# A Fourier mixing layer and an MLP in one kernel: outputs of a pair of products one product later, the last stage's first splits tied to tiles 10 to 12, and one block's scale from ScalarE's sums

## The chip, the cores and the metric

The kernel runs on one core of a Trainium2 chip. That core has a matrix engine (TensorE, in the profile PE for its matmuls and PEld for its weight loads), three engines for elementwise work (VectorE or DVE, ScalarE or ACT, GpSimd or POOL) and SyncE (SP), which only issues transfers here. Every engine works through its own queue in order. The metric is the device time of one execution in microseconds; the time before is 1283.4 us, the median of 3 runs (1282.92 to 1283.59).

## What is computed

The input x has 2048 rows of 576 numbers. It is normalized row by row, and the result goes through a Fourier mixing layer and an MLP, whose outputs are added to x:

```
xn = layernorm(x)
a  = xn @ dft_hid_re.T          b = xn @ dft_hid_im.T
y  = dft_seq_re @ a - dft_seq_im @ b        # 2048 x 2048 matrices
h  = relu(xn @ w1)                          # 576 -> 4608
out = x + y + h @ w2                        # 4608 -> 576
```

All data are float32.

## The kernel before

**Numbers as two halves.** TensorE works on float16. Each float32 operand is scaled by a power of two and split in a high half (ScalarE, a copy to float16) and a low half (VectorE, the scaled value minus the high half). A product of two such operands is three matmuls: low by high, high by high, high by low. `split` (lines 182 and 183) is this pair of instructions. The scale of an operand comes from its largest value, or from a sum of absolute values, which bounds it: from VectorE's reduction (`magnitude`, L115) or from ScalarE's accumulator (`sum_w1`, L578; `sum_w2`, L604). `power_pe` finds the maximum over partitions with two small matmuls (L158 and L166), `power` does it with GpSimd.

**Strassen's scheme.** Most large products are done as 2 x 2 blocks with seven products P1 to P7 in place of eight; the sums and differences that this needs are VectorE's work.

**The stages.** First a prologue loads x, normalizes and transposes it and starts the MLP. Then the main loop goes over 9 blocks of w1 and w2 (512 hidden units each) and, in each block, over 4 groups of 512 rows. Blocks 0 and 1 form the hidden values with plain products (L310). From block 2 on, 28 steps form them as two "pairs" of seven products each (`pair_products`, L440): the loop names them first and second. A product's result lies in one of four PSUM banks. Some products have a copy or an add that frees the bank for the next one (the table `free`, L466 to L471), and some have outputs that are not needed in this step (the table `use`): `value`, L447 and L448, makes the two halves of an output, P3 finishes r21 (L476), P4 makes A12 and the four sums (L451 to L454). Two more instructions split these sums at the end: L459 on ScalarE and L462 on VectorE, held in a list `ends`. Between those products stand the seven products of the second matrix (`mlp2`, L510) of the step before, which read the hidden values h; L519 and L521 take their results out, and GpSimd adds them to DRAM (L523). After the MLP comes the hidden transform, 16 tiles of 128 rows (`dft1`, L1002 and L1012), whose results are split into R (L1022 to L1034). The last stage multiplies the 2048 x 2048 matrices with R: 16 units of seven products (L1116), each with an operand of 128 x 1024 that `operand` forms by adds and subtracts (L1063 to L1068) and a split.

**Preparing.** A list `todo` holds small steps of preparation: for each block of weights the loads, the scale, the sums and the splits; before the last stage `power_c` (the scale), `load_c(0)` and the first three operands. `work()` takes one entry off, and the loops call it at fixed places (`ready` in the paired steps; once after each tile from tile 2 on in the transform). A second list, `passes`, loads each block of the 2048 x 2048 matrices once ahead of time and sums its absolute values on ScalarE (L874), one entry at each `count`.

**What sets the order.** The builder lays out each engine's queue before the run. It goes through the instructions on its own model of the machine: an engine that is free there takes, among those that are ready by that model, the one that stands first in the program's text. So an instruction can run ahead of its place in the text where the model saw the engine idle. `tc.issue_after(ins)` forbids that: what is traced inside it on the engine of `ins` comes behind `ins` in the queue. The dictionary `order` keeps the instructions used for this: `order["s"]` and `order["lo"]` are the last closing splits (L459 and L462 in the paired steps), `order["acc"]` is the last accumulation (L521).

The order of a paired step is written out by hand as a list of (what, which) in lines 919 to 927.

Of the kernel before, what the change touches and what calls it, by code (L numbers as in the profile page):

```python
# [2 lines left out]

# [6 lines left out]
F16 = mybir.dt.float16  # L10
F32 = mybir.dt.float32
BF16 = mybir.dt.bfloat16
I32 = mybir.dt.int32
AF = mybir.ActivationFunctionType
ALU = mybir.AluOpType
# [3 lines left out]
P = 128  # L19
# [11 lines left out]
GH = G // 2  # L31
KT = 5
# [10 lines left out]
BB = 2  # L43
# [6 lines left out]
def kernel(  # L50
# [17 lines left out]
    nc = tc.nc  # L68

    const = ctx.enter_context(tc.tile_pool(name="const", bufs=1))  # L70
    small = ctx.enter_context(tc.tile_pool(name="small", bufs=2))
# [3 lines left out]
    mlp = tc.alloc_tile_pool(name="mlp", bufs=2)  # L75
# [17 lines left out]
    raws = {}  # L93
# [19 lines left out]
    def magnitude(dst, src):  # L113

        nc.vector.tensor_reduce(dst, src, AX.XY, ALU.max, apply_absolute_value=True)  # L115
# [72 lines left out]
    means, factors, shifts, order = {}, {}, {}, {}  # L188
# [115 lines left out]
    w1s, w2s, us, hs = {}, {}, {}, {}  # L304
    w1bufs = [mlp.tile([P, W1B], F32, name=f"w1buf{i}", bufs=1) for i in range(2)]
# [61 lines left out]
    P1, P2, P6, P5, P7, P3, P4 = range(7)  # L367
# [161 lines left out]
    sc, pw, mx = {}, {}, {}  # L529

    def max_w1(b, f):

        i, r = divmod(f, 2)
        if f == 0:
            mx["w1", b], sc["w1", b], pw["w1", b] = cell("mw1"), cell("sw1"), cell("pw1")
        if r == 0:
            mx["f", b] = cell("mf", 2)
            mx["b", i] = small.tile([P, 1], BF16, tag=f"mb{i}", name=f"mb{b}_{i}")
        with tc.issue_after(order["lo"]) if b else nullcontext():
            magnitude(mx["f", b][:, r : r + 1], raws["w1", b, i][:, r * KT : (r + 1) * KT])  # L540
        if r:
            nc.vector.tensor_reduce(mx["b", i], mx["f", b], AX.X, ALU.max)

# [28 lines left out]
    def sum_w1(b, i):  # L572

        if i == 0:
            mx["w1", b], sc["w1", b], pw["w1", b] = cell("mw1"), cell("sw1"), cell("pw1")
        w = w1bufs[b % 2 * 2 + i].bitcast(F16)
        w1s[b, i] = w.rearrange("p (n k f) -> p n k f", n=2, f=P)
        nc.scalar.activation(  # L578
            w[:, : 2 * KT * P].rearrange("p (k f) -> p k f", f=P), raws["w1", b, i], AF.Abs,
            scale=2.0**-10, accum_out=mx["w1", b][:, i : i + 1],  # L580
        )

    def sums_w1(b, i):
        r = raws["w1", b, i]
# [65 lines left out]
    def prepare_w1(b, i):  # L650
        p = power_w1(b, i)
        if b < BB:
            return [
                lambda: max_w1(b, 2 * i),
                lambda: max_w1(b, 2 * i + 1),
                lambda: later(p),
            ], [
                lambda: split_w1(b, 2 * i),
                lambda: split_w1(b, 2 * i + 1),
            ]  # L660
        return [
            lambda: (sum_w1(b, i), next(p)),
            lambda: None,
            lambda: later(p),
        ], [
            lambda: split_w1b(b, i, 0),
            lambda: split_w1b(b, i, 1),
            lambda: sums_w1(b, i),
            lambda: split_w1b(b, i, 2),
            lambda: split_w1b(b, i, 3),  # L670
        ]
# [91 lines left out]
    w = prepare_w2(0)  # L763
# [118 lines left out]
    for n in range(2, len(steps)):  # L882
        b, g = steps[n]
        pb, pg = steps[n - 1]
        if g == 0 and b:
            if b + 1 < NB:
                todo += prepare_block(b + 1)
            else:
                todo += [lambda: (load_d(0), load_d(1)), lambda: None, new_d, lambda: None]
                for j in range(4):  # L890
                    d = power_d(j)
                    todo += [lambda d=d: next(d), lambda d=d, j=j: (later(d), split_d(j))]
                    if j < 2:
                        todo += [lambda j=j: load_d(j + 2), lambda: None]
                todo += [scales_d]
        if b == 0 and g + 1 < NG:
            with tc.issue_after(order["lo"]):
                weave(stats([(g + 1) * TG + i for i in range(TG)]))
        if b == NB - 1 and g:

            size = 2 * EH
            if g == 1:
                w = mlp.tile([P, 2, 7, EH], F16, tag="w2s", name="sums", bufs=4)
                w = [w.rearrange("p n q e -> p (n q e)").bitcast(F32)]
            elif g == 2:
                w = [raw.tile([P, KT, EH], F32, tag="raw", name=f"sums{k}") for k in range(2)]
                w = [r.rearrange("p k e -> p (k e)") for r in w]
            sumbufs[:] = [
                r[:, k : k + size].rearrange("p (c e) -> p c e", e=EH)
                for r in w for k in range(0, r.shape[1] - size + 1, size)  # L910
            ]
        if b >= BB:
            first, second = (pair_products(b, g, i) for i in range(NQ))
            later1, later2 = (lambda q, f=f: f(q, True) for f in (first, second))
            m = lambda q: mlp2(pb, pg, q)
            end = lambda q: ends and ends.pop(0)()
            ready = lambda q: [work() for _ in range(q)]
            count = lambda q: n > 3 and passes and passes.pop(0)()
            for do, q in (
                (first, P1), (first, P2), (m, 0), (end, 0), (first, P6), (ready, 1),  # L920
                (first, P5), (later1, P2), (ready, 1), (m, 1), (end, 0), (second, P1), (ready, 1),
                (first, P7), (m, 2), (second, P2), (later1, P7), (ready, 1),
                (first, P3), (first, P4), (count, 0), (later1, P3), (m, 3), (later1, P4), (second, P6),
                (later2, P2), (ready, 1), (m, 4), (end, 0), (second, P5), (ready, 1), (m, 5), (end, 0),
                (second, P7), (ready, 1), (m, 6), (ready, 2), (second, P3), (later2, P7),
                (count, 0), (second, P4), (later2, P3), (later2, P4), (ready, 1),
            ):
                do(q)
            for _ in range(4):
                next(tq, None)  # L930
            continue
        ps = []
        for i in range(NF):
            if n == 2:
                ps.append(early.pop(0) if early else mlp1(b, g, i))
            else:
                mlp1_step(b, g, i, ps)
            if i % 2:
                mlp1_out(b, g, i // 2, *ps[i - 1 : i + 1])
            if b == 0 and g + 1 < NG:  # L940
                t = (g + 1) * TG + i
                normalize(t)
                remainder(t, nc.gpsimd)
                transposes(t)
            if n == 2 and i == 2:
                todo += prepare_block(1)
            for _ in range(1 if b else 3):
                work()
            for q in range(2 * i, min(2 * i + 2, 7)):
                mlp2(pb, pg, q)  # L950
                if b:
                    next(tq, None)
            if b and i == 3:
                next(tq, None)
            for _ in range(1 + i % 2 if b else 3):
                work()
            if n > 3 and i % 2 and passes:
                passes.pop(0)()
# [30 lines left out]
    def dft1(t):  # L989
# [40 lines left out]
            nc.scalar.activation(hi, src, AF.Copy, scale=r)  # L1030
            stt(lo, src, r, hi, ALU.mult, ALU.subtract)  # L1031
        hi, lo = (R[t][:, n, T3 : T2 + 1] for n in range(2))
        nc.scalar.activation(hi, T, AF.Copy)
        nc.vector.tensor_tensor(lo, T, hi, ALU.subtract)  # L1034

    A = {}

    def load_c(n):
        pool = cr[n % 2]
        for q, src in enumerate(blocks_c(n)):  # L1040
            r = A[n, q] = pool.tile([P, HK, P], F32, tag=f"c{q}", name=f"c{q}_{n}")
            nc.sync.dma_start(r, src)
# [13 lines left out]
    def operand(m):  # L1056

        n, i = divmod(m, 7)
        q = PRODUCTS[i][0]
        a11, a22, a12, a21 = (A[n, j] for j in range(4))  # L1060
        tt = nc.vector.tensor_tensor
        if q == S2:
            tt(a21, a21, a22, ALU.add)  # L1063
            tt(a11, a21, a11, ALU.subtract)
        elif q == S3:
            tt(a21, a22, a11, ALU.subtract)
        elif q == S4:
            tt(a12, a12, a11, ALU.subtract)  # L1068
        src = {A11: a11, A22: a22, A12: a12, S1: a21, S2: a11, S3: a21, S4: a12}[q]
        w = csp[m] = cs.tile([P, 2, HK, P], F16, tag="cs", name=f"cs{m}")  # L1070
        split(w[:, 0], w[:, 1], src, sc["c"][:, n : n + 1])

    todo += [power_c, lambda: None, lambda: load_c(0)] + [lambda: None] * 8
    todo += [lambda m=m: operand(m) for m in range(3)]
    for t in range(NT):
        if t and t % TG == 0:
            xpool[t // TG - 1].release()
# [104 lines left out]
```

## Time and profile before

| | |
|---|---|
| median of 3 runs | 1283.4 us |
| the profiled execution | 1285.6 us |
| its span, first to last instruction | 1283.8 us |
| mean granted TensorE clock | 0.995 |
| paired steps (blocks 2 to 8) | about 206 to 836 us |
| transform | about 836 to 949 us |
| last stage | about 949 us to the end |

The profile comes from one execution. A row of a group of instructions gives line, engine, operation, what it writes and reads, shapes and count, then busy time and mean duration, then the engine's idle time just before these instructions and what ended it. A row of the timeline gives start, length and instruction, with the idle time before it in brackets. A row of the waits gives who waited for whom, the total in us, how often, and the longest. A row of windows gives for each stretch the busy time of each engine with its count of instructions, the granted clock of TensorE and the transfers' share. Matmuls are pipelined: their number in a stretch says more about TensorE's pace than its busy time.

### The profile page before, as it was taken

The numbers are of one execution on the slowest core, as the hardware profiler recorded it, in microseconds if no ns is written. First come the engines' busy times: TensorE is split into PE (matmuls) and PEld (weight loads), VectorE is DVE, ScalarE is ACT, GpSimd is POOL, SyncE is SP. The second block draws the span as 40 slices with busy tenths as digits, with TensorE's granted clock in tenths as the row PEclk, the third lists the DMA queues.
The fourth block names the chain that finished last, engine by engine and source line by source line (L and its number), as shares of the span: only waits on it lengthen the run. The fifth ranks groups of instructions, "written<-read, shape, count | busy, mean of one in ns | idle before, by whom it ended". The sixth has DMA issues, their size and how long they took to land.

```text
span 1283.8 us, 25483 instructions
## 1 busy us (share of the span) xinstructions
PE 1247.0 (97%) x10396; PEld 990.4 (77%) x10396; DVE 1002.9 (78%) x1879; ACT 727.8 (57%) x1218; POOL 149.0 (12%) x188
## 2 busy tenths in 40 slices
PE   7899999999999999999999999999999999999998
PEld 7665566888888888878878887867777777777776
DVE  8989998786877776777867877567668788888875
ACT  5835567676776676766766765544443333333332
POOL 2320012111112121211121111100000000000000
PEclk9899999999999999999999999999999999999999
DMA  6112457566756675666666665630033435344320
GB/s 242 43 62 69 124 124 153 131 116 142 146 131 122 133 149 121 133 136 126 120 142 143 138 135 121 111 94 17 1 124 113 153 105 165 117 127 135 127 85 20
DMA packets 60806, 150.75 MB, mean 117 GB/s; under 512 B 6288, under 2 KB 21136, under 8 KB 60688
## 3 DMA queue, kind: packets, MB, share of 16 engines
q1 hardware_dynamic: 42256, 111.36, 27.1%
q0 software_dynamic: 18432, 37.76, 20.9%
q8 instruction: 81, 1.33, 0.4%
q14 instruction: 37, 0.30, 0.1%
HBM read 101.91 MB, written 47.19 MB: 116 GB/s over the span
## 4 chain that ended last, share of the span: by engine, by line
PE 69%; DVE 17%; ACT 5%; DMA 5%; issue 3%; SPq 1%; POOL 0%; ACTq 0%; POOLq 0%; DVEq 0%
PE p L1116 25%; PE p L510 17%; PE bank L440 17%; PE pd L1002 7%; DMA raw_w<-in_w_dram 2%; DVE w2s L183 2%; PE p L310 2%; ACT h L459 1%; DVE h L448 1%; DVE h L462 1%; ACT f L874 1%; DMA c<-in_cim_dram 1%; DMA c<-in_cre_dram 1%; DVE dbuf L183 1%; DVE w1buf L183 1%
## 5 line engine op out<-in xcount | busy, mean ns | idle before, releaser
L510 PE MATMUL p<-w2s,h 128*128 128x288 f16 x3024 | 409.8, 286 | 4.7 <-DVE acc L521 2.0
L510 PEld LDWEIGHTS <-h 128*128 128x128 f16 x3024 | 295.0, 98 | 81.3 <-issue 6.1
L1116 PE MATMUL p<-R,cs 128*128 128x288 f16 x2688 | 329.6, 286 | 1.8 <-DVE o L1122 1.8
L1116 PEld LDWEIGHTS <-cs 128*128 128x128 f16 x2688 | 263.0, 98 | 68.2 <-issue 2.0
L182 ACT ACTIVATE cs<-c,sc_c 128x1024 f16<-128x1024 f32 x112 | 128.5, 1148 | 205.1 <-PE p L1116 151.3
L183 DVE SCALAR_TENSOR_TENSOR cs<-c,sc_c,cs 128x1024 f16<-128x1024 f32 x112 | 143.7, 1283 | 50.9 <-ACT cs L182 50.8
L440 PEld LDWEIGHTS <-w1buf 128*128 128x128 f16 x1600 | 156.4, 98 | 30.4 <-issue 9.3
L440 PEld LDWEIGHTS <-dbuf 128*128 128x128 f16 x1200 | 117.3, 98 | 22.7 <-issue 7.0
L440 PE MATMUL bank<-xT,w1buf 128*128 128x256 f16 x832 | 109.8, 273 | 1.9 <-ACT acc L469 1.9
L1002 PE MATMUL pd<-dbuf,xT 128*128 128x288 f16 x832 | 106.0, 289 | 2.4 <-DVE R L1031 2.4
L440 PE MATMUL bank<-acc,w1buf 128*128 128x256 f16 x768 | 102.1, 272 | 4.6 <-DVE acc L470 2.9
L462 DVE TENSOR_TENSOR h<-s,h 128x1024 f16<-128x1024 f32 x56 | 68.5, 1224 | 48.4 <-ACT h L459 48.4
L1002 PEld LDWEIGHTS <-xT 128*128 128x128 f16 x832 | 81.5, 99 | 25.8 <-issue 4.8
L523 POOL DMA_DIRECT2D spill<-dbuf x74 | 64.1, 868 | 291.9 <-DVE dbuf L521 225.8
L440 PE MATMUL bank<-xT,dbuf 128*128 128x256 f16 x624 | 82.3, 273 | 1.6 <-ACT acc L469 1.6
L447 ACT ACTIVATE h<-acc 128x256 f16<-128x256 f32 x112 | 46.3, 414 | 59.9 <-DVE acc L470 43.6
L440 PE MATMUL bank<-acc,dbuf 128*128 128x256 f16 x576 | 76.6, 272 | 3.1 <-ACT s L468 1.7
L448 DVE SCALAR_TENSOR_TENSOR h<-acc,h 128x256 f16<-128x256 f32 x112 | 47.3, 423 | 35.1 <-ACT h L447 34.8
L1122 DVE SCALAR_TENSOR_TENSOR o<-p,us_c,o 128x288 f32<-128x288 f32 x112 | 57.5, 514 | 20.3 <-PE p L1116 20.3
L459 ACT ACTIVATE h<-s 128x1024 f16<-128x1024 f32 x56 | 59.0, 1053 | 20.9 <-DVE s L454 19.6
L874 ACT ACTIVATE f<-f 128x1024 f32<-128x1024 f32 x64 | 67.1, 1049 | 5.1 <-DMA f<-in_cre_dram 5.1
L519 ACT ACTIVATE dbuf<-p,c_ub 128x576 f32<-128x576 f32 x74 | 54.1, 732 | 21.4 <-ACT h L447 11.3
(158 smaller groups left out, 1538.7 us busy)
## 6 DMA issues: line engine op xcount, KB each, us to landing
spill<-dbuf POOLq DMA_DIRECT2D x74, 288.0 KB, 5.2
f<-in_cre_dram SPq DMA_DIRECT2D x32, 512.0 KB, 4.5
f<-in_cim_dram SPq DMA_DIRECT2D x32, 512.0 KB, 3.7
c<-in_cre_dram SPq DMA_DIRECT2D x32, 512.0 KB, 4.6
c<-in_cim_dram SPq DMA_DIRECT2D x32, 512.0 KB, 4.8
spill<-sum POOLq DMA_DIRECT2D x38, 288.0 KB, 5.2
raw_w<-in_w_dram SPq DMA_DIRECT2D x17, 640.0 KB, 5.0
raw_w<-in_w_dram SPq DMA_DIRECT2D x18, 576.0 KB, 3.8
```

What stands on the lines that cost most here:

```text
L182: nc.scalar.activation(hi, src, AF.Copy, scale=s)
L183: nc.vector.scalar_tensor_tensor(lo, src, s, hi, ALU.mult, ALU.subtract)
L440: nc.tensor.matmul(ps, l, r, start=first and m == 0, stop=m == len(todo) - 1, skip_group_check=not first,)
L448: stt(lo, src, 0.0, hi, ALU.max, ALU.subtract)
L459: order["s"] = nc.scalar.activation(hi_s, st[:, 1:], AF.Copy).ins
L462: order["lo"] = nc.vector.tensor_tensor(lo_s, st[:, 1:], hi_s, ALU.subtract).ins
L510: nc.tensor.matmul(ps[:, c], h[:, x, qa, c * P : (c + 1) * P], w[:, y, qb], start=first and i == 0 and j == 0, stop=i == NQ - 1 and j == 2 ...
L523: nc.gpsimd.dma_start(spill[g, row, col], o, accum_op=ALU.add)
L874: nc.scalar.activation(f, f, AF.Abs, scale=2.0**-10, accum_out=sums_c[:, n, q : q + 1])
L1002: nc.tensor.matmul(ps[j], xT[g][:, kx, c * P : (c + 1) * P], dsp[j][:, hl, k], start=(t % 2 == 0 and n == 0), stop=(t % 2 == 1 and n == le ...
L1116: nc.tensor.matmul(ps, w[:, a, k], r[:, c, rq], start=first and k == 0 and j == 0, stop=k == HK - 1 and j == 2, skip_group_check=not first,)
L1122: nc.vector.scalar_tensor_tensor(o, ps, us["c"][:, n : n + 1], o, ALU.mult, ALU.add)
```

## The change

Three places change.

The scale of block 1's w1 no longer comes from VectorE's two reductions per half (`max_w1`), which stood behind `order["lo"]`, but from `sum_w1`, so far used from block 2 on; in block 1 it writes its junk output to a tile of the ring "stage", and a copy to bfloat16 hands the sums to `power_pe`. The preparing list keeps its length.

In the paired step, the outputs of the first pair (`later1`) and of the second (`later2`), the closing splits (`end`) and the second `count` change places with products and preparing entries.

In the transform, each tile now records its closing splits in `order`, the empty entries ahead of the first three operands go from 8 to 5, and those operands are tied behind the closing splits of the tile after which they are called.

```diff
 def max_w1(b, f):
-        with tc.issue_after(order["lo"]) if b else nullcontext():
-            magnitude(mx["f", b][:, r : r + 1], raws["w1", b, i][:, r * KT : (r + 1) * KT])
+        magnitude(mx["f", b][:, r : r + 1], raws["w1", b, i][:, r * KT : (r + 1) * KT])
...
 def sum_w1(b, i):
-        w = w1bufs[b % 2 * 2 + i].bitcast(F16)
-        w1s[b, i] = w.rearrange("p (n k f) -> p n k f", n=2, f=P)
+        if b < BB:
+            junk = mlp.tile([P, 5, GH], F32, tag="stage", name=f"j1_{b}_{i}")
+            junk = junk.rearrange("p a b -> p (a b)")
+        else:
+            junk = w1bufs[b % 2 * 2 + i].bitcast(F16)
+            w1s[b, i] = junk.rearrange("p (n k f) -> p n k f", n=2, f=P)
         nc.scalar.activation(
-            w[:, : 2 * KT * P].rearrange("p (k f) -> p k f", f=P), raws["w1", b, i], AF.Abs,
+            junk[:, : 2 * KT * P].rearrange("p (k f) -> p k f", f=P), raws["w1", b, i], AF.Abs,
             scale=2.0**-10, accum_out=mx["w1", b][:, i : i + 1],
         )
+        if b < BB:
+            mx["b", i] = small.tile([P, 1], BF16, tag=f"mb{i}", name=f"mb{b}_{i}")
+            nc.vector.tensor_copy(mx["b", i], mx["w1", b][:, i : i + 1])
...
 def prepare_w1(b, i):
-                lambda: max_w1(b, 2 * i),
-                lambda: max_w1(b, 2 * i + 1),
+                lambda: sum_w1(b, i),
+                lambda: None,
                 lambda: later(p),
...
                 (first, P1), (first, P2), (m, 0), (end, 0), (first, P6), (ready, 1),
                 (first, P5), (later1, P2), (ready, 1), (m, 1), (end, 0), (second, P1), (ready, 1),
-                (first, P7), (m, 2), (second, P2), (later1, P7), (ready, 1),
-                (first, P3), (first, P4), (count, 0), (later1, P3), (m, 3), (later1, P4), (second, P6),
-                (later2, P2), (ready, 1), (m, 4), (end, 0), (second, P5), (ready, 1), (m, 5), (end, 0),
-                (second, P7), (ready, 1), (m, 6), (ready, 2), (second, P3), (later2, P7),
-                (count, 0), (second, P4), (later2, P3), (later2, P4), (ready, 1),
+                (first, P7), (m, 2), (second, P2), (ready, 1), (first, P3), (first, P4), (count, 0),
+                (later1, P7), (m, 3), (second, P6), (later1, P3), (later1, P4), (later2, P2),
+                (ready, 1), (m, 4), (second, P5), (ready, 1), (m, 5), (end, 0), (second, P7),
+                (end, 0), (ready, 1), (m, 6), (count, 0), (ready, 2), (second, P3), (second, P4),
+                (later2, P7), (later2, P3), (later2, P4), (ready, 1),
...
 def dft1(t):
-        nc.scalar.activation(hi, T, AF.Copy)
-        nc.vector.tensor_tensor(lo, T, hi, ALU.subtract)
+        order["s"] = nc.scalar.activation(hi, T, AF.Copy).ins
+        order["lo"] = nc.vector.tensor_tensor(lo, T, hi, ALU.subtract).ins
...
-    todo += [power_c, lambda: None, lambda: load_c(0)] + [lambda: None] * 8
-    todo += [lambda m=m: operand(m) for m in range(3)]
+    todo += [power_c, lambda: None, lambda: load_c(0)] + [lambda: None] * 5
+    def first_operand(m):
+        with tc.issue_after(order["s"]), tc.issue_after(order["lo"]):
+            operand(m)
+
+    todo += [lambda m=m: first_operand(m) for m in range(3)]
```

More of the change, by code (lines that the diff above doesn't have):

```diff
@@ L1 @@
 import itertools
-from contextlib import ExitStack, nullcontext
+from contextlib import ExitStack
 import concourse.bass as bass
```

## The prediction

> **What bounds the kernel now.** I read the page first: its span, the engines' shares, and its stages by windows; then the list of waits on TensorE, and last the timeline wherever that list names a place. The page:
>
> ```profile
> span 1283.8 us, 25483 instructions
> ...
> PE 1247.0 (97%) x10396; PEld 990.4 (77%) x10396; DVE 1002.9 (78%) x1879; ACT 727.8 (57%) x1218; POOL 149.0 (12%) x188
> ```
>
> TensorE is busy for 1247.0 of 1283.8 us, so whatever this change can win lies in 36.8 us of idle time and in any slow matmuls; no edit adds or removes work of TensorE. Three stages hold the edits of loop and last stage (window, its length, PE busy, PEld, DVE, ACT, POOL, granted clock, DMA share, GB/s):
>
> ```profile
> 206.00:750.00 544.00, 535.43 (x4588) 448.52 (x4587) 410.97 (x905) 377.74 (x733) 93.37 (x119) 1.00 0.65 135
> 750.00:836.00 86.00, 83.26 (x711) 69.09 (x710) 60.52 (x125) 50.70 (x93) 16.65 (x20) 1.00 0.58 116
> 836.00:949.00 113.00, 110.64 (x906) 84.73 (x904) 77.32 (x129) 50.53 (x81) 2.62 (x3) 0.98 0.12 32
> ```
>
> The paired steps (206 to 836) idle TensorE 8.6 + 2.7 = 11.3 us, the transform (836 to 949) 2.4 us at a clock below 1.00. TensorE's waits by releaser (total, times, longest):
>
> ```profile
> PE bank L440 <- DVE acc L470: 4.0, 8, 1.4
> PE bank L440 <- ACT acc L469: 3.5, 5, 1.1
> ...
> PE pd L1002 <- DVE R L1031: 2.4, 3, 1.3
> PE bank L440 <- ACT s L468: 2.2, 3, 1.2
> ...
> PE p L1116 <- DVE o L1122: 1.8, 1, 1.8
> PE p L310 <- ACT xT L265: 1.5, 2, 1.2
> ...
> PE pm L158 <- DVE mb L614: 0.4, 1, 0.4
> ...
> PE pm L158 <- DVE mb L542: 0.2, 1, 0.2
> ```
>
> L440 is the paired steps' products, L1002 the transform, L1116 the last stage; L310 and L158 are the first products and the scales of blocks 0 and 1.
>
> **Part 1, the last stage's first splits.** Their 3 entries come after 5 empty ones instead of 8, so in the text they move from tiles 13, 14, 15 to tiles 10, 11, 12; and they may no longer run ahead of that place. Today they do. The timeline at the transform's start:
>
> ```profile
> 848.75 1.15 ACT L182 ACTIVATE cs<-c,sc_c 128x1024 f16<-128x1024 f32 x1 [2.81 <-DMA c<-in_cim_dram]
> 849.81 0.87 ACT L1030 ACTIVATE R<-pd,c_rho 128x288 f16<-128x288 f32 x2
> ...
> 850.89 0.28 PE L1002 MATMUL pd<-dbuf,xT 128*128 128x288 f16 x1 [0.45 <-DVE R L1031]
> ...
> 851.74 0.28 PE L1002 MATMUL pd<-dbuf,xT 128*128 128x288 f16 x1 [0.57 <-DVE R L1031]
> ...
> 853.36 5.38 PE L1002 MATMUL pd<-dbuf,xT 128*128 128x288 f16 x29 [1.34 <-DVE R L1031]
> ```
>
> ScalarE stands 2.81 us in front of a split whose matrix block has not landed; tile 0's evacuation (L1030) is queued behind it; TensorE wants tile 0's four banks for tile 2 and waits three times, 0.45 + 0.57 + 1.34 = 2.4 us. Then it runs slowly:
>
> ```profile
> 850.00:858.00 8.00, 5.64 (x31) 3.52 (x30) 7.65 (x11) 3.62 (x6) 0.00 (x0) 0.79 0.00 0
> 858.00:948.00 90.00, 90.00 (x752) 69.56 (x751) 66.29 (x114) 43.17 (x71) 0.00 (x0) 1.00 0.02 7
> ...
> 853.30:858.10 4.80, 4.74 (x26) 3.21 (x26) 4.77 (x7) 1.10 (x2) 0.00 (x0) 0.64 0.00 0
> ```
>
> Undisturbed, 752 matmuls take 90 us, 0.120 each. In the 8 us from 850 there are 31 where 8.00 / 0.120 = 67 belong: 36 x 0.120 = 4.3 us lost, the 2.4 of waits and about 1.9 at a granted clock of 0.64. With the splits gone from here nothing is late: tile 0's evacuation is then ACT and DVE work of its own tile only, as in every later tile.
>
> What covers the splits at their new place? Tile 10, and the price of a split and of one add or subtract:
>
> ```profile
> 917.97 1.17 DVE L1031 SCALAR_TENSOR_TENSOR R<-pd,c_rho,R 128x288 f16<-128x288 f32 x2
> ...
> 919.67 1.36 DVE L1034 TENSOR_TENSOR R<-T,R 128x1152 f16<-128x1152 f32 x1 [0.53 <-ACT R L1033]
> ...
> 922.43 0.52 DVE L1024 SCALAR_TENSOR_TENSOR T<-pd,c_rho,c 128x288 f32<-128x288 f32 x1 [1.40 <-ACT c L1022]
> ```
>
> ```profile
> L183 DVE SCALAR_TENSOR_TENSOR cs<-c,sc_c,cs 128x1024 f16<-128x1024 f32 x112 | 143.7, 1283 | 50.9 <-ACT cs L182 50.8
> ...
> L1063 DVE TENSOR_TENSOR c<-c,c 128x1024 f32<-128x1024 f32 x16 | 19.5, 1221 | 4.5 <-DMA c<-in_cre_dram 3.4 <-DMA c<-in_cim_dram 0.8
> ```
>
> VectorE ends tile 10 at 921.03 and waits 1.40 us for tile 11: a split of 1.28 fits. The banks give more room: the last read of tile 10's banks ends at 919.14, and tile 12, which reuses them, starts when tile 11 is done, by 921.9: about 2.7 us. Operand 2 brings two adds and a split, 2 x 1.22 + 1.28 = 3.7 us; less 1.40 it delays tile 13 by 2.3, inside the 2.7. Cost 0; without that cover up to 3.3 us (rival 2). I take -4.3; ends -4.3 and -1.0. The added order puts each split behind its tile's L1033 on ScalarE and L1034 on VectorE; the next tile's L1022 and L1024 queue behind it, and behind those TensorE two tiles on.
>
> The Trainium skill bears on the slow stretch ("TensorE: Matmul & The Clock Gate", section "Why this matters for your kernels"): it asks for no idle gaps over about 3 us, since a window of idleness halves the clock. The longest gap here is 1.34 us and the clock still fell, so page and trace differ, and the measurement decides; by the page alone only the 2.4 us of waits would come back, and the whole sum would be 1280.4.
>
> **What the moved work releases.** The subtracts of operands 4 and 5, which also run early today, can only follow operand 2; so the first block's buffer comes free later, and SP issues the load that refills it for the third unit later, next to the second unit's four loads. The last stage has one wait, which hangs on loads:
>
> ```profile
> 963.70 1.23 DVE L1063 TENSOR_TENSOR c<-c,c 128x1024 f32<-128x1024 f32 x1 [3.45 <-DMA c<-in_cre_dram]
> ```
>
> VectorE stands at the second unit's add until its block lands, with the output add L1122 queued behind it and TensorE behind that (1.8 us above). Another load in front would lengthen it; a VectorE that is later at that add would let L1122 by. Between +1.8 (TensorE's wait once more) and -1.8 (L1122 let by); I take 0, the row as it stands.
>
> **Part 2, block 1's scale.** Durations (groups by line), and an idle stretch of ScalarE on the timeline:
>
> ```profile
> L578 ACT ACTIVATE w1buf<-raw_w 128x1280 f16<-128x1280 f32 x8 | 10.1, 1264 | 9.4 <-DMA raw_w<-in_w_dram 9.4
> ...
> L115 DVE TENSOR_REDUCE c_mf<-raw_w 128x1 f32<-128x640 f32 x8 | 6.3, 804 | 0.0
> ...
> L542 DVE TENSOR_REDUCE mb<-c_mf 128x1 bf16<-128x2 f32 x4 | 0.6, 143 | 0.0
> ...
> L614 DVE CAST mb<-c_mw 128x2 bf16<-128x2 f32 x2 | 0.3, 158 | 0.7 <-ACT j L604 0.7
> ```
>
> ```profile
> 71.51 0.87 ACT L243 ACTIVATE dbuf<-acc,sh,r 128x576 f16<-128x576 f32 x1 [3.47 <-DVE sh L222]
> ```
>
> Half of the eight reductions are block 1's. VectorE loses 4 x 0.80 + 2 x 0.14 and gains 2 x 0.16: -3.2 us; ScalarE gains 2 x 1.26 = 2.5 us and a short read of each accumulator. ScalarE has gaps such as the 3.47 us before 71.51; its new junk comes from the two "stage" buffers that L350 and L604 also take. TensorE gains only where it waits for that maximum: 0.2 (L542), and 0.4 (L614: second w2 load, which starts when block 1's second split is done). Taken: -0.6. Ends: -1.8 (those 0.6 and L310's one wait of 1.2, for transposed x that stood behind a split of this block), and +1.3, one sum in front of an evacuation with nothing to cover it.
>
> **Part 3, the paired step.** Nothing is added. In the text the first pair's A22 value, its other outputs and its two closing splits (L459, L462) come after the next product's copy; the load and sum of a matrix block (L874; one 512 KB load on SP each) and one preparing entry swap places with them. No POOL work moves. The order of the queues is not the text's, though:
>
> ```profile
> 272.63 1.06 ACT L459 ACTIVATE h<-s 128x1024 f16<-128x1024 f32 x1
> 273.60 0.36 ACT L468 ACTIVATE s<-bank 128x256 f32<-128x256 f32 x1
> 273.86 1.05 ACT L874 ACTIVATE f<-f 128x1024 f32<-128x1024 f32 x1
> ```
>
> Before the change the text has L468 (second, P6) ahead of L459, and the queue has them the other way round: what the builder held to be ready first went first. Where TensorE does wait, in the fourth group of a block:
>
> ```profile
> 298.40 1.04 ACT L459 ACTIVATE h<-s 128x1024 f16<-128x1024 f32 x1
> 299.35 1.04 ACT L874 ACTIVATE f<-f 128x1024 f32<-128x1024 f32 x1
> ...
> 300.39 0.36 ACT L469 ACTIVATE acc<-bank 128x256 f32<-128x256 f32 x1
> ```
>
> L469, second P5's copy, for which TensorE waits, comes 2.1 us late behind L459 and L874. The new text puts it ahead of L459. But L874 stood behind L469 in the old text already and still went first, so L469 was not held ready there, and a new place in the text changes nothing. I take 0. Ends: -3.5 (all five waits on L469 gone) and rival 3's loss.
>
> **Sum.** -4.3 + 0 - 0.6 + 0 = -4.9 us. The profiled execution took 1285.6, its span and 1.8 around it, and would take 1280.7; the median of the runs, 1283.4, lies 2.2 under it, so the forecast is 1278.5.
>
> **Rivals.** *1, the paired step gains* (0.18): L469 goes first, -3.5 more: 1275.0. For it: five equal places. Against it: L874's order.
> *2, the stall moves to the transform's end or the last stage's loads* (0.15): operand 2, the fourth split and two more subtracts, 3.7 + 1.28 + 2 x 1.22 = 7.4 us, all in front of tile 13's evacuation; less 1.40 and 2.7 that is 3.3 us: 1281.8, no measurable change. Against it: tile 13's evacuation is ready before the last of these.
> *3, slower* (0.10): the second pair's outputs come late for the next step's third product.
>
> ```profile
> 264.77 1.23 DVE L462 TENSOR_TENSOR h<-s,h 128x1024 f16<-128x1024 f32 x1 [0.79 <-ACT h L459]
> ...
> 266.02 0.78 PE L510 MATMUL p<-w2s,h 128*128 128x288 f16 x5
> ```
>
> L462 ends at 266.00; that product needs it at its fifth matmul, 266.02 + 4 x 0.12 = 266.5. Half a us of room: if the second L874, now earlier in the text, runs ahead of that chain, it costs 1.05 - 0.5 = 0.55 us in each of 28 steps, 15 us: 1293.9. It decides from 0.5 us on. Against it: at 273.86 L874 ran well before that chain.
>
> **How the numbers follow.** The forecast's case has 0.57. A measurement here tells about 0.2%, 2.6 us: faster means under 1280.8. Faster: 0.57 and 0.18, with 0.02 of rival 2; the other 0.13 of it is "same"; rival 3 is slower: 0.77, 0.13, 0.10. The range, 1273.5 to 1284, reaches from rival 1 with part 2's better end to rival 2 with part 2's worse one, and leaves out rival 3.
>
> **What would show it.** Right: no wait on L1031 around 850 and a clock of 1.00 there; the first split beginning after tile 10's L1033; waits on L469 as before (3.5). Wrong: waits on L1031 near 940, a longer wait on L1122 near 961, L510 waiting for L462 in every step, or ScalarE standing in front of an early sum between 60 and 75.

## The result, and the profile after

The changed kernel takes 1276.9 us (median of six runs, 1275.4 to 1277.6) against 1283.5 for the kernel before, run beside it. The ratio is 0.9945, with a 95% interval of 0.9931 to 0.9958: faster by 0.4 to 0.7%. The forecast was 1278.5 in a range of 1273.5 to 1284. The profiled execution took 1277.3 us, its span 1275.5.

The code moved: in the changed kernel the transform's products are L1008 and L1018, its evacuation L1036 and L1037, its closing splits L1039 and L1040, the last stage's products L1126 and output add L1132, its adds L1069 to L1074, the sum of a matrix block L880, the sum for w1's scale L581. The page, and then the stages by windows (columns as before):

```profile
span 1275.5 us, 25491 instructions
...
PE 1242.4 (97%) x10396; PEld 987.9 (77%) x10396; DVE 998.6 (78%) x1875; ACT 730.1 (57%) x1222; POOL 149.2 (12%) x188
```

```profile
206.00:750.00 544.00, 536.01 (x4605) 450.28 (x4604) 409.90 (x903) 379.29 (x735) 93.64 (x119) 1.00 0.64 135
750.00:832.00 82.00, 80.49 (x686) 66.73 (x685) 58.26 (x121) 47.85 (x89) 17.49 (x21) 1.00 0.61 121
832.00:940.00 108.00, 107.41 (x894) 82.85 (x893) 75.34 (x128) 50.37 (x80) 1.86 (x3) 1.00 0.12 29
```

The transform is now 108 us with 0.6 us of idle TensorE, where it was 113 with 2.4 and a clock of 0.98 (these windows begin and end at rounded times; the table below goes by matmuls). TensorE's waits:

```profile
PE bank L440 <- ACT acc L469: 3.9, 5, 0.9
...
PE bank L440 <- DVE acc L470: 2.6, 7, 0.4
...
PE p L1126 <- DVE o L1132: 1.7, 2, 1.5
...
PE bank L440 <- ACT s L468: 1.0, 1, 1.0
...
PE pm L158 <- DVE acc L521: 0.9, 1, 0.9
PE pd L1008 <- DVE R L1037: 0.6, 2, 0.4
...
PE p L310 <- ACT xT L265: 0.3, 1, 0.3
```

Against the list of before: the evacuation's wait fell from 2.4 to 0.6, that on L470 from 4.0 to 2.6, that on L265 from 1.5 to 0.3; the two waits on the scale of w1 and w2 (0.2 and 0.4) are gone and one of 0.9 stands at L158. The waits on L469 and on the output add are about what they were. The wait on L468 fell from 2.2 to 1.0, but it differs from execution to execution: the kernel before has none in its second trace.

TensorE's 10396 matmuls are the same in every kernel here, and so is their order, but for part 2, which moves the small matmuls of block 1's scale among those of blocks 0 and 1. So the length of a stretch can be taken between the starts of the same two matmuls, counted from the first, in each trace. The cuts lie near the changes of stage, not on them. In us:

| stretch | before | after | difference |
|---|---|---|---|
| prologue (to matmul 600) | 59.9 | 58.5 | -1.4 |
| blocks 0 and 1 (600 to 1517) | 147.0 | 145.7 | -1.3 |
| paired steps (1517 to 6816) | 630.3 | 628.2 | -2.1 |
| transform (6816 to 7708) | 111.6 | 108.0 | -3.6 |
| last stage (7708 to the last matmul) | 331.1 | 331.2 | +0.1 |

The prologue has no part in the change. Over all the traces it is 57.9 to 60.4 us long, at a granted clock of 1.00 to 0.89 in its first 60 us. Its 1.4 us, which belong to these two executions, are most of why the spans differ by 8.3 us and the medians only by 6.6.

### The profile page after: what moved, and what is told of

Read it like the earlier page. It is cut to its first block, busy times and chain, and to the rows that moved or that the text cites. A ratio compares the mean times of both kernels' runs of the same rounds, so it can differ in the third digit from the quotient of the medians.

```text
span 1275.5 us, 25491 instructions
## 1 busy us (share of the span) xinstructions
PE 1242.4 (97%) x10396; PEld 987.9 (77%) x10396; DVE 998.6 (78%) x1875; ACT 730.1 (57%) x1222; POOL 149.2 (12%) x188
## 4 chain that ended last, share of the span: by engine, by line
PE 62%; DVE 20%; DMA 8%; ACT 6%; issue 4%; POOL 1%; SPq 0%; ACTq 0%; POOLq 0%; DVEq 0%
PE p L1126 23%; PE bank L440 15%; PE p L510 15%; PE pd L1008 7%; DMA raw_w<-in_w_dram 3%; DVE w2s L183 2%; DMA f<-in_cre_dram 1%; PE p L310 1%; DVE h L448 1%; ACT f L880 1%; DVE h L462 1%; ACT h L459 1%; DVE acc L521 1%; DMA spill<-sums 1%; DVE h L354 1%
## 5 line engine op out<-in xcount | busy, mean ns | idle before, releaser
L1126 PE MATMUL p<-R,cs 128*128 128x288 f16 x2688 | 329.8, 286 | 1.7 <-DVE o L1132 1.7
L1126 PEld LDWEIGHTS <-cs 128*128 128x128 f16 x2688 | 263.0, 98 | 68.3 <-issue 2.0
L440 PEld LDWEIGHTS <-w1buf 128*128 128x128 f16 x1600 | 156.5, 98 | 29.1 <-issue 8.1
L440 PEld LDWEIGHTS <-dbuf 128*128 128x128 f16 x1200 | 117.4, 98 | 21.4 <-issue 5.8
L440 PE MATMUL bank<-xT,w1buf 128*128 128x256 f16 x832 | 109.9, 273 | 2.7 <-ACT acc L469 2.6
L462 DVE TENSOR_TENSOR h<-s,h 128x1024 f16<-128x1024 f32 x56 | 68.5, 1223 | 48.8 <-ACT h L459 48.8
L440 PE MATMUL bank<-acc,w1buf 128*128 128x256 f16 x768 | 102.1, 272 | 2.8 <-DVE acc L470 1.5
L1008 PE MATMUL pd<-dbuf,xT 128*128 128x288 f16 x832 | 104.1, 286 | 0.6 <-DVE R L1037 0.6
L1008 PEld LDWEIGHTS <-xT 128*128 128x128 f16 x832 | 80.7, 98 | 22.9 <-issue 2.9
L440 PE MATMUL bank<-xT,dbuf 128*128 128x256 f16 x624 | 82.3, 273 | 1.4 <-ACT acc L469 1.4
L440 PE MATMUL bank<-acc,dbuf 128*128 128x256 f16 x576 | 76.6, 272 | 2.5 <-DVE acc L470 1.1
L1132 DVE SCALAR_TENSOR_TENSOR o<-p,us_c,o 128x288 f32<-128x288 f32 x112 | 57.4, 512 | 20.1 <-PE p L1126 19.5
L459 ACT ACTIVATE h<-s 128x1024 f16<-128x1024 f32 x56 | 59.0, 1053 | 22.5 <-DVE s L454 21.3
L880 ACT ACTIVATE f<-f 128x1024 f32<-128x1024 f32 x64 | 67.2, 1050 | 5.4 <-DMA f<-in_cre_dram 5.4
```

The costliest lines, as they stand in the source:

```text
L440: nc.tensor.matmul(ps, l, r, start=first and m == 0, stop=m == len(todo) - 1, skip_group_check=not first,)
L459: order["s"] = nc.scalar.activation(hi_s, st[:, 1:], AF.Copy).ins
L462: order["lo"] = nc.vector.tensor_tensor(lo_s, st[:, 1:], hi_s, ALU.subtract).ins
L880: nc.scalar.activation(f, f, AF.Abs, scale=2.0**-10, accum_out=sums_c[:, n, q : q + 1])
L1008: nc.tensor.matmul(ps[j], xT[g][:, kx, c * P : (c + 1) * P], dsp[j][:, hl, k], start=(t % 2 == 0 and n == 0), stop=(t % 2 == 1 and n == le ...
L1126: nc.tensor.matmul(ps, w[:, a, k], r[:, c, rq], start=first and k == 0 and j == 0, stop=k == HK - 1 and j == 2, skip_group_check=not first,)
```

## The experiments

### The kernel before once more, and each part alone

The first kernel is the one before, unchanged. The others have one of the three parts of the change's diff each.

> The kernel before, unchanged, for a second profile of it. If the slow clock near 853 us (0.64) belongs to the waits, it is there again, and TensorE's waits on L1031 are 2.4 us again. If it depends on where the clock's own period happens to stand, the waits stay and the slow stretch is absent or shorter.

> Only the transform's part: the three operands moved and tied, the rest as before. Theory (prediction, part 1): the 4.3 us around 850 us come back, less the 0.9 us of waits that the changed kernel still shows there, so 3.4 us faster, ratio 0.9973. Rival a: the slow clock after the three waits is not there in every execution, then 1.5 to 2 us faster, 0.9986. Rival b: this part is the whole gain, 6.6 us, 0.9948.

> Only block 1's scale from the sums. Theory (part 2): 0.6 to 1.0 us faster, ratio 0.9993, with the first matmul of block 1 about 1 us earlier against the work before it; no wait of TensorE on an early sum. Rival: the sums cost ScalarE more than VectorE wins, 1 us slower, 1.0008.

> Only the new text of the paired step. Theory (part 3): the queues are filled by what the builder holds ready, so the time between 206 and 836 us changes by less than 0.5 us, ratio 1.0000, and L469 keeps its five waits. Rival: the closing split L462 behind second P7's add and the later outputs bring 2 to 3 us, 0.9980, as the stage is that much shorter in the changed kernel's profile.

| kernel | median, us | before beside it | ratio, 95% interval | that is, us |
|---|---|---|---|---|
| unchanged (one run) | 1283.4 | | | |
| part 1, transform | 1279.4 | 1284.1 | 0.9962 (0.9949 to 0.9975) | -4.9 |
| part 2, scale | 1283.0 | 1284.1 | 0.9992 (0.9981 to 1.0004) | -1.0 |
| part 3, paired step | 1282.4 | 1284.1 | 0.9990 (0.9979 to 1.0001) | -1.3 |

The three add up to -7.2, the whole change to -7.1 (0.0055 of 1283.5). The intervals are about 1.5 us wide to each side, so part 1's gain is certain by itself and the others' are not. The lengths between the same matmuls are steadier. The transform has 111.1 to 112.9 us in the three kernels without part 1 and 107.7 with it. Blocks 0 and 1 have 147.0 to 147.4 without part 2, and 146.2 with it alone. Over all the traces of this document the transform has 111.1 to 113.6 us without part 1's tie, and blocks 0 and 1 have 146.8 to 147.8 without part 2 and 144.6 to 146.2 with it. In part 2's kernel the waits of TensorE show the same exchange as in the changed kernel:

```profile
PE pm L158 <- DVE acc L521: 0.9, 1, 0.9
...
PE p L310 <- ACT xT L265: 0.3, 1, 0.3
```

### Part 1: its place or its tie

```diff
-    todo += [power_c, lambda: None, lambda: load_c(0)] + [lambda: None] * 8
+    todo += [power_c, lambda: None, lambda: load_c(0)] + [lambda: None] * 5
```

> The kernel before with 5 empty entries in place of 8, and no added order. Theory: the place in the text means nothing here, the splits run ahead in both; the first split still stands for its block's landing near 844 us, TensorE still loses 3.5 to 5 us between 845 and 860 (waits on L1031 and, in some executions, the slow clock), the transform from its first to its last matmul keeps 111 to 113 us. Rival: the place alone is enough, about 108 us.

The other half keeps the eight empty entries and takes the tie alone:

```diff
+        order["s"] = nc.scalar.activation(hi, T, AF.Copy).ins
+        order["lo"] = nc.vector.tensor_tensor(lo, T, hi, ALU.subtract).ins
...
+        with tc.issue_after(order["s"]), tc.issue_after(order["lo"]):
+            operand(m)
```

> The added order, but the splits left at tiles 13 to 15. Theory: the order is what works, so the transform takes 107.5 to 108.5 us as with both; the last stage then starts its first products with operands 2 and 3 not yet made (operand 2 behind tile 15: two adds and a split, 4.9 us after about 6 us of tile 15's own work, wanted 5.9 us into the stage), so it should lose 3 to 6 us there. Rival: the last stage takes the same 330 to 331 us.

The new place alone took 1289.1 us against 1284.7 beside it, one run. Its transform is 111.5 us long, as before. The 4 us more lie elsewhere: the paired steps took 631.4 us, and the last stage 333.1, where the granted clock fell once more (0.50 from 967.39 to 970.80). TensorE's wait in the transform has the row of before:

```profile
PE pd L1002 <- DVE R L1031: 2.4, 3, 1.3
```

The tie alone has a transform of 107.8 us and a last stage of 335.0, where it was 331.1. The whole took 1284.4, no gain (TensorE's waits; here L1120 is the last stage's product):

```profile
PE p L1120 <- ACT cs L182: 4.2, 2, 3.6
...
PE pd L1002 <- DVE R L1031: 0.4, 1, 0.4
```

So the tie removes the stall, and the earlier place is needed so that the splits are not late for the last stage. Either half alone gained nothing.

### Part 3: which of its moves

In the one kernel only the two closing splits of the first pair move, L459 from behind the second matrix's product 4 to behind product 5, and L462 from there to behind second P7. In the other kernel everything else moves. The edit of the one:

```diff
-   (later2, P2), (ready, 1), (m, 4), (end, 0), (second, P5), (ready, 1), (m, 5), (end, 0),
-   (second, P7), (ready, 1), (m, 6), ...
+   (later2, P2), (ready, 1), (m, 4), (second, P5), (ready, 1), (m, 5), (end, 0),
+   (second, P7), (end, 0), (ready, 1), (m, 6), ...
```

> The kernel before with only the two closing splits of the first pair moved (behind m5 and behind second P7). Theory: of the paired step's edit only this matters: L470's longest wait falls from 1.4 to 0.4 us and its total from 4.0 to 2.6, as in the changed kernel. Rival: L470 keeps its 4.0.

> The kernel before with the paired step's other moves (outputs of both pairs, the second matrix sum) and the closing splits where they were. Theory: nothing, L470's waits stay at 4.0 with the 1.4 among them, L469's between 3.5 and 4.6. Rival: the outputs bring the 1.4 us back, L470 at 2.6.

TensorE's waits, first of the kernel with the closing splits moved, then of the other one:

```profile
PE bank L440 <- ACT acc L469: 3.9, 5, 1.0
...
PE bank L440 <- DVE acc L470: 2.4, 7, 0.4
```

```profile
PE bank L440 <- DVE acc L470: 3.9, 8, 1.3
PE bank L440 <- ACT acc L469: 3.4, 5, 1.1
```

Both times were those of the kernel before (1284.2 and 1284.5; one run each can't tell 1 us). The place can be named, though: of the 28 paired steps, 184 matmuls each from the first of L440 (matmul 1576), one differs by kernel and not by run. Number 25 of 0 to 27 is 22.2 to 22.5 us long in all six traces with the moved closing splits and 23.7 to 24.0 in all seven without. The timeline of that step, of the kernel before and then of the changed one:

```profile
780.42 1.22 DVE L462 TENSOR_TENSOR h<-s,h 128x1024 f16<-128x1024 f32 x1
...
781.55 1.72 DVE L183 SCALAR_TENSOR_TENSOR dbuf<-raw_d,c_sd,dbuf 128x1440 f16<-128x1440 f32 x1
...
783.18 0.42 DVE L470 TENSOR_TENSOR acc<-bank,acc 128x256 f32<-128x256 f32 x1
...
783.66 0.60 PE L440 MATMUL bank<-acc,w1buf 128*128 128x256 f16 x4 [1.36 <-DVE acc L470]
```

```profile
776.81 0.41 DVE L470 TENSOR_TENSOR acc<-bank,acc 128x256 f32<-128x256 f32 x1
...
777.14 1.21 DVE L462 TENSOR_TENSOR h<-s,h 128x1024 f16<-128x1024 f32 x1
```

Before, second P7's add L470 stood behind the closing split L462 and a split of 1.72 us for the transform's matrix. Now it goes ahead of both, and the wait of 1.36 us is gone. No other effect of part 3 was found: the remaining steps differ between runs of one kernel by as much as between kernels.

### What is left at the transform's start

The changed kernel still waits there, twice:

```profile
844.03 0.89 ACT L1036 ACTIVATE R<-pd,c_rho 128x288 f16<-128x288 f32 x2 [4.74 <-DMA spill<-sums]
844.57 0.52 DVE L1037 SCALAR_TENSOR_TENSOR R<-pd,c_rho,R 128x288 f16<-128x288 f32 x1 [3.88 <-ACT R L1036]
...
845.99 0.28 PE L1008 MATMUL pd<-dbuf,xT 128*128 128x288 f16 x1 [0.21 <-DVE R L1037]
846.65 0.53 PE L1008 MATMUL pd<-dbuf,xT 128*128 128x288 f16 x3 [0.38 <-DVE R L1037]
```

ScalarE is no longer held by a split but by a transfer: R's buffer holds the last sums until they are written to DRAM. That transfer was issued at 834.02 and landed at 843.93, among four loads of c that SP issued from 833.0 to 834.9. The edit issues those loads later, from ScalarE:

```diff
-            nc.sync.dma_start(r, src)
+            if n:
+                nc.sync.dma_start(r, src)
+            else:
+                with tc.issue_after(order["s"]):
+                    nc.scalar.dma_start(r, src)
```

> The changed kernel, with the four loads of the last stage's first unit (c) issued by ScalarE behind the closing split of transform tile 4 in place of SyncE near 833. What it tests: why 0.6 us of waits on L1037 are left at 846 in the changed kernel, where ScalarE's L1036 stands 4.7 us for the last spill transfer. Theory (the four c loads, issued 833.0 to 834.9, share the transfers with the spill issued at 834.0 and make it land late): the spill lands 2 to 5 us sooner, L1036 waits under 2.5 us, no wait of TensorE on L1037 near the transform's start; the c blocks land near 880, still ahead of tile 10's splits; transform and last stage otherwise as they are, 0.5 to 1 us shorter in all. Rival (the spill is late by itself): L1036 waits 4 to 5 us as before and the waits on L1037 stay at 0.6.

The spill took from 835.93 to 841.59, 5.7 us in place of 9.9, and ScalarE does not wait for it (timeline):

```profile
841.79 0.50 ACT L1036 ACTIVATE R<-pd,c_rho 128x288 f16<-128x288 f32 x1 [0.58 <-DVE T L1030]
```

No wait on L1037 is left, the transform is 107.05 us long, 0.9 less, and the loads, issued from 870.4, had landed by 880.4. The first theory held. The whole took 1277.8 us, not less than the changed kernel's 1276.9: the paired steps of that run, which the edit does not reach, were 1.8 us longer.

### Why the copies L469 come late

The forecast put L469 behind L459 and L880 (then L874). In the changed kernel:

```profile
295.11 1.27 ACT L581 ACTIVATE w1buf<-raw_w 128x1280 f16<-128x1280 f32 x1 [2.62 <-DMA raw_w<-in_w_dram]
...
296.38 1.04 ACT L459 ACTIVATE h<-s 128x1024 f16<-128x1024 f32 x1
297.32 1.04 ACT L880 ACTIVATE f<-f 128x1024 f32<-128x1024 f32 x1
...
298.36 0.36 ACT L469 ACTIVATE acc<-bank 128x256 f32<-128x256 f32 x1
...
298.77 0.49 PE L440 MATMUL bank<-xT,w1buf 128*128 128x256 f16 x3 [0.83 <-ACT acc L469]
```

Ahead of both stands the sum of the next block's w1, taken ahead of its place in the text, and ScalarE waits 2.62 us for its weights to land. The edit ties the sums from block 2 on behind the closing split on ScalarE:

```diff
+        with tc.issue_after(order["s"]) if b >= BB else nullcontext():
             nc.scalar.activation(
                 junk..., raws["w1", b, i], AF.Abs, scale=2.0**-10, accum_out=mx["w1", b][:, i : i + 1],
             )
```

> The changed kernel, with the sums for w1's scale from block 2 on (L581) tied behind the closing split, so that they can't run ahead of their place. What it tests: why the five waits on L469 (3.9 us) were not touched by the paired step's new order. Theory (ScalarE takes this sum early, stands 2 to 3 us for its weights to land, and L459, L880 and L469 come late one after the other): the five waits on L469 fall to under 0.5 us, the paired steps are 3 to 4 us shorter than the 628 to 630 us of the kernels so far, the whole time about 3.5 us less than the changed kernel. Rival (L469 is late because of L459 and L880 alone, whatever stands before them): the waits stay between 2.5 and 4 us; or the later sum makes the scale and the next block's split late, which shows as new waits on the scale's small matmul (L158) or on ScalarE's split, and the time does not fall.

It took 1269.3 us in one run, 7.6 under the changed kernel. The timeline at the same step, and TensorE's waits in all the paired steps, which are these two rows and no more:

```profile
292.91 1.06 ACT L459 ACTIVATE h<-s 128x1024 f16<-128x1024 f32 x1 [1.53 <-DVE s L454]
293.87 1.04 ACT L881 ACTIVATE f<-f 128x1024 f32<-128x1024 f32 x1
...
294.91 0.36 ACT L469 ACTIVATE acc<-bank 128x256 f32<-128x256 f32 x1
...
304.04 1.27 ACT L582 ACTIVATE w1buf<-raw_w 128x1280 f16<-128x1280 f32 x1
```

```profile
PE bank L440 <- DVE acc L470: 2.6, 7, 0.4
PE bank L440 <- DVE s L471: 0.9, 1, 0.9
```

L469 still comes behind L459 and the matrix block's sum, and nobody waits for it: neither of these two made it late, the stand in front of them did. The paired steps are 621.0 us long, 7.2 less, twice what the theory expected. The five steps in which L469 was waited for are 0.96 to 1.18 us shorter, 5.4 together, more than the 3.9 of their waits; part of it is 0.14 us that each of them lost again at the L470 behind. One step is shorter by 1.2 us, where TensorE had waited for L468 behind a spill; three others give the remaining 0.5. In this run and the next no wait on L468 is left. That need not be the tie's doing: the second trace of the kernel before has none either, and the same step took 21.2 us there as here. So 5.4 us of the 7.2 are shown, and the rest stays open.

### All of it

To both edits a third is added: in the last stage the second add or subtract for the next unit's operand goes behind the output add.

```diff
-                operand(m + AHEAD)
+                with tc.issue_after(order["o"]) if i == 6 else nullcontext():
+                    operand(m + AHEAD)
...
-            nc.vector.scalar_tensor_tensor(o, ps, us["c"][:, n : n + 1], o, ALU.mult, ALU.add)
+            order["o"] = nc.vector.scalar_tensor_tensor(
+                o, ps, us["c"][:, n : n + 1], o, ALU.mult, ALU.add
+            ).ins
```

> The changed kernel with the two edits above and a third: in the last stage the second add or subtract of the next unit's first operand is tied behind the output add (L1132) that stood in the queue behind it. Theory: the waits of TensorE on L1037 (0.6), L469 (3.9) and L1132 (1.7) go, 6.2 us together, and the time falls from 1276.9 to about 1271, a ratio to the kernel before of 0.990 (0.988 to 0.992). Rivals: only the sum's part comes back, 1273 (0.992), since the output add then makes the next operand late by what it gained; or the tied sum delays the scale and nothing is gained over the changed kernel (0.9945).

The median is 1266.6 us (four runs, 1265.6 to 1267.3) against 1284.3 beside it, a ratio of 0.9866 (0.9849 to 0.9882). That is faster than either kernel, and faster than any of the theories had it, mostly because the tied sum came with about twice its price. The paired steps have 620.8 us, the transform 107.1, the last stage 329.2 in place of 331.2. No run has the third edit alone. Without it the wait on the output add is 0.7 to 1.9 us and the last stage 330.0 to 331.2 in the traces (but for the two in which the clock fell in that stage), so the edit's share is an estimate of 0.8 to 2.0 us. Where TensorE had waited for the output add, its timeline has one unbroken row:

```profile
939.76 15.48 PE L1132 MATMUL p<-R,cs 128*128 128x288 f16 x125
```

## Why the prediction was right, step by step

**Part 1 (forecast -4.3, found -3.6 to -3.9 in the transform).** The stall went, and the clock with it. The three operands run where they were put: each split begins behind its tile's closing split. Operand 2's adds and split fall into tile 13's evacuation: the closing split L1040 of tile 13 starts at 933.80, 9.1 us behind tile 12's, where 6.7 are usual. So it is some 2.3 us late, as the forecast had it, and TensorE does not wait, up to 940 (timeline of the changed kernel: tile 10, tile 13's closing split, and then the second unit's add in the last stage):

```profile
910.10 1.16 ACT L1039 ACTIVATE R<-T 128x1152 f16<-128x1152 f32 x1
911.16 1.14 ACT L182 ACTIVATE cs<-c,sc_c 128x1024 f16<-128x1024 f32 x1
911.29 1.36 DVE L1040 TENSOR_TENSOR R<-T,R 128x1152 f16<-128x1152 f32 x1 [0.54 <-ACT R L1039]
912.57 1.28 DVE L183 SCALAR_TENSOR_TENSOR cs<-c,sc_c,cs 128x1024 f16<-128x1024 f32 x1
...
933.80 1.35 DVE L1040 TENSOR_TENSOR R<-T,R 128x1152 f16<-128x1152 f32 x1
...
955.02 1.23 DVE L1069 TENSOR_TENSOR c<-c,c 128x1024 f32<-128x1024 f32 x1 [3.11 <-DMA c<-in_cre_dram]
```

```profile
842.00:850.00 8.00, 7.41 (x60) 5.65 (x59) 4.75 (x9) 3.54 (x7) 0.00 (x0) 1.00 0.29 112
850.00:940.00 90.00, 90.00 (x752) 69.55 (x751) 68.89 (x116) 45.59 (x72) 0.00 (x0) 1.00 0.01 1
```

From 850 on 752 matmuls take 90 us, the pace that the forecast took for undisturbed. In the 8 us before there are 60 where 67 belong, 7 x 0.120 = 0.8 us lost, and that is about what the gain falls short of 4.3. The step that failed is "nothing is late" with the splits gone: the spill of the last sums is late next. With it out of the way the transform is 107.05 us, 4.5 less than before, beside the 4.3 of the forecast.

The split of these 4.3 in 2.4 of waits and 1.9 of slow clock is the other step that failed: the slow clock did not cost its 1.9. The clock did not always fall (last section), and with a full clock the transform was nearly as long. The first of the three waits differs, 0.3 to 1.8 us. Less that wait, the transform is 110.8 us long in the three executions with a full clock, 111.0 to 111.1 in the three that lost 1.7 us to the clock once, and 111.9 in the one that lost it twice. With a full clock TensorE outruns the late evacuation once more, as with part 2 alone (timeline; three matmuls in 1.13 us behind another wait):

```profile
858.49 1.13 PE L1018 MATMUL pd<-dbuf,xT 64*128 64x288 f16 x3 [0.38 <-DVE R L1037]
```

So a loss of 1.7 us to the clock cost 0.2 to 0.3 us there; the evacuation's lag set the pace. The sum was right because it counted the matmuls that were missing and not only the waits.

**What the moved work releases (0, found 0.0).** The third unit's load is issued at 940.05, where it was at 870.23, and so 4.8 us ahead of the second unit's loads, as the forecast had it. The wait on the output add is 1.7 us as against 1.8; over the traces without the tie it is 1.0 to 2.1 and with place and tie 0.7 to 1.7, so an effect under 1 us would not show.

**Part 2 (forecast -0.6, found -0.9 to -1.3).** The two waits on the scale went, as priced, though the 0.4 on L614 is missing in two traces without part 2 as well. The wait of 1.2 at L310, which the forecast kept for the better end, went too; a wait of 0.9 on L521 that it did not have came: -0.6 - 1.2 + 0.9 = -0.9. ScalarE does not stand in front of the new sums.

**Part 3 (forecast 0, found -1.5 in one step).** The failed step is "a new place in the text changes nothing". It holds for L469, from which it was argued. It was not examined for VectorE's L470, though the first row of the waits shown, 4.0 us with a longest of 1.4, stood there. The queue had kept the text's order at this place, and the move changed it.

**The rivals.** The measured 1276.9 us lies about midway between the forecast and rival 1's 1275.0, so the time alone does not tell them apart; the waits do. Rival 1 did not come about: the five waits on L469 stayed. Its gain was to be had, and larger than its price of 3.5, but from the early sum, whose row the forecast shows ("9.4 <-DMA raw_w<-in_w_dram") and does not connect. Rival 2 would have shown waits near 940, and there are none. Rival 3 would have shown products waiting for L462, and no such row exists.

**The sum.** The forecast has -4.9, and the runs -6.6 by the medians. Of the difference, part 3's 1.5 us is the largest term. Part 1 brought 0.4 to 0.7 us less than forecast and part 2 0.3 to 0.7 more; that these two cancel is luck.

## What to carry to other kernels

An instruction that was pulled forward in an in-order queue and waits there for a transfer costs the work queued behind it, on that engine and on those that wait for it. The idle column of the groups shows it as "DMA", and the wait that TensorE shows names another instruction: follow the engine's timeline back from the late instruction to the last stand. Tie the pulled instruction behind one that must come first, and see that its new place is still early enough for its user: for the last stage's splits each half alone gained nothing.

Take a stretch's price from the matmuls missing in it, and compare variants between the same matmuls. That told 1.5 us in one step, where the totals of single runs could not.

## What the runs showed of the hardware

The granted clock around the stalled start of the transform differs between executions of the same instructions there. The same 28 us, 838 to 866, in the kernel before, with part 2 alone, and with the closing splits moved (windows; the clock is the third number from the end):

```profile
838.00:866.00 28.00, 25.64 (x198) 18.85 (x197) 18.21 (x28) 12.10 (x19) 1.15 (x2) 0.94 0.40 106
```

```profile
838.00:866.00 28.00, 25.14 (x202) 18.54 (x201) 20.10 (x31) 12.88 (x20) 0.00 (x0) 1.00 0.33 97
```

```profile
838.00:866.00 28.00, 24.50 (x182) 17.47 (x181) 20.00 (x31) 12.95 (x19) 0.00 (x0) 0.88 0.29 87
```

And 10 us of the prologue, in the kernel before:

```profile
30.00:40.00 10.00, 7.34 (x99) 6.97 (x95) 7.60 (x27) 7.60 (x15) 7.04 (x9) 0.83 0.01 2
```

The loss comes in equal portions: 0.06 x 28 = 1.7 us, 0.12 x 28 = 3.4, 0.17 x 10 = 1.7. One portion, cut out of the kernel before, is 3.41 us at a clock of 0.50 (second row; the first row is the stretch ahead of it):

```profile
851.11:854.52 3.41, 1.50 (x12) 1.03 (x11) 3.41 (x6) 1.94 (x3) 0.00 (x0) 1.00 0.00 0
854.52:857.93 3.41, 3.41 (x16) 2.17 (x15) 3.38 (x6) 0.93 (x1) 0.00 (x0) 0.50 0.00 0
```

The changed kernel, the one with part 1 alone and the one with the tie alone, whose TensorE waits 0.4 to 0.6 us there, have 1.00. The Trainium skill ("TensorE: Matmul & The Clock Gate", section "What's actually happening") says that the clock is either full or half, by a free-running window of 3.4 us. The trace agrees: 1.7 us lost is 3.4 us at half clock. Where the windows begin differs between executions, and so does how much of the three waits falls into one. In the four executions whose clock fell here, TensorE was busy for 1.2 to 1.5 us of the 3.41 us ahead of it. Between the half-clock stretches that begin at 35.32 and 854.52 in the kernel before lie 240 steps of 3.413 us. Cut in such steps, counted from another half-clock stretch of the same trace, the emptiest window of the three that stayed full has 1.6 to 2.2 us. This is no sharp limit: at the end of the kernel with all the edits (1258.35 to 1261.76) a window with 1.4 us is followed by a clock of 1.00. The Trainium skill's rule on the same page (section "Why this matters for your kernels"), no idle gap over some 3 us, names too long a gap for this place: with none over 1.8 us the clock fell in four executions and stayed full in three.

A transfer of 288 KB from GpSimd's queue took 9.9 us among four loads of 512 KB and 5.7 without them.
